# One PSUM tensor of eight banks in place of two rings, a shared exp/mask buffer and a new order, in a windowed attention with a folded feed-forward

## The chip, the cores and the metric

The kernel runs on one core of one Trainium2 chip. The metric is the device time of one launch in microseconds (us); the time given for a kernel is the median of its runs.

## The reference

Sliding-window attention with four sink tokens, and behind it a feed-forward with a product of two branches. Batch 4, 8 heads, 768 positions, head dimension 64; model width 512, inner width 1024; the attention's output, 3072 rows of 512, is the feed-forward's input. Inputs and output are float32.

```python
scores = scale * np.matmul(q, k.transpose(0, 1, 3, 2))
is_sink = pos[None, :] < int(n_sink)              # n_sink = 4
rel = pos[:, None] - pos[None, :]
in_window = (rel >= 0) & (rel < int(window))      # window = 128
scores = np.where(is_sink | in_window, scores, -1000000000.0)
a = np.exp(scores - np.max(scores, axis=-1, keepdims=True))
a = a / (np.sum(a, axis=-1, keepdims=True) + 1e-09)
attn = np.matmul(a, v)
x = attn.transpose(0, 2, 1, 3).reshape(B * S, H * D)
out = (((x @ w1) * (x @ w2)) @ w3) @ w_out
```

## The kernel before, in words

**Tiling.** A batch `b` has 768 positions: three tiles `t` of 256 queries, or six blocks `kb` of 128. The eight heads form four pairs `r`. Products run in bf16 with float32 sums. Because nothing stands between w3 and w_out, the kernel first folds them into one matrix, w3 @ w_out (`w3o`).

**The tasks on TensorE.** Each is a small generator whose first step issues the matmuls and whose later steps issue what other engines do with the result. The plan names them so:

- `t3.i.j`: `fold_w3`, transposes of row block `i` of w3 (line 402). Blocks 0 to 2 come as raw float32 over SP (line 173) and are transposed in two halves of four; the others come through POOL as bf16 (line 131) and take one task of eight transposes.
- `fm.i.n`: `fold_mm`, block `i` of w3 times 128 columns of w_out (line 413), eight matmuls. The four column slices 0 to 3 of w_out are loaded one by one, as ("wo", 0, 128), ("wo", 128, 256) and so on.
- `tpk`, `tpq`: transposes of k and q. Batch 0 uses `transposes_paired` (line 261), two tiles of batch 1 `transposes` (line 233). All later ones are DMA transposes that SP issues (`transposes_dma`, line 270), two for each block: one of k, one of q.
- `sc.b.r.t`: `scores`, the products of k and q of two heads for 256 queries in a tile of two PSUM banks (line 309). ScalarE takes the exponential (line 317), VectorE multiplies with a mask (line 321). Some of these tasks also make the scores of the sink keys (line 303), for two query tiles at once in batches 2 and 3.
- `av.b.r.t`: `values`, probabilities times v, with the row sum in a 65th column (line 343); VectorE takes the reciprocal and scales (lines 347 and 350).
- `sv.b`: `sink_values`, the v rows of the sinks (line 284).
- `xt.b.r.t`: `x_transposes`, transposes of the attention's result (line 360). From batch 1's last tile on, DMA transposes from SP do it (line 370).
- `g.b.c.dt.h`: `gate`, one 128-row block of the first (`h` = 0) or second (1) branch over a chunk `c` of 256 or 384 positions (line 383). ScalarE copies the first branch out into `a_sb` (line 390), VectorE multiplies the second with it (line 387).
- `p.b.m`: `project`, 128 rows of output from `ab` and `w3o` (line 423), copied out by ScalarE or VectorE and stored by SP (line 430). The last one is done in three pieces (`project_pieces`, line 440).

**What sets the order.** `PLAN` lists all 337 TensorE tasks, and TensorE takes them exactly so. The orders of ScalarE, VectorE and SP come out of a small planner that runs while the kernel is built. It gives each step a duration and each load a due time (`arrive`, corrected by `LATER` for batches 2 and 3), and lets each engine take what is ready first. Nothing is decided on the chip: every engine runs its list in order and waits where an input is missing. POOL issues its loads in the order of the list `order`, then q, k and v of batches 1 to 3; no more than eight of its transfers are outstanding.

**PSUM.** There are two pools. `ps_sc` is a ring of two tiles of two banks, for scores alone. `ps_mm` is a ring of four tiles of one bank, for everything else. A ring hands its slots out in turn, so that a task waits for the slot used two, or four, tasks earlier.

**SBUF.** The exponential goes into a tile `ex` (three buffers) and the masked result into a tile `am` (four buffers).

**Filling at the start.** Where the planner sees TensorE idle in the first 40 us, `keep_busy` puts in matmuls whose result is not used (line 458).

Of the kernel before, what the change touches and what calls it, by code (L numbers as in the profile page):

```python
# [21 lines left out]
def kernel(  # L22
# [47 lines left out]
    ps_sc = ctx.enter_context(tc.tile_pool(name="ps_sc", bufs=2, space=PSUM))  # L70
    ps_mm = ctx.enter_context(tc.tile_pool(name="ps_mm", bufs=4, space=PSUM))
# [52 lines left out]
    def load(what, *i):  # L124
# [18 lines left out]
        else:  # L143
# [5 lines left out]
    order = [("w3", 3), ("w3", 4), ("wo", 0, 128), ("wo", 256, 384), ("wo", 384, 512), ("w3", 7), ("q", 0, 0),  # L149
             ("k", 0, 0), ("w3", 6), ("wo", 128, 256), ("k", 0, 1), ("v", 0, 0), ("q", 0, 1), ("q",  # L150
             0, 2), ("w3", 5), ("v", 0, 1), ("k", 0, 2), ("w2", 768, 1024), ("w1", 768, 1024),
             ("w2", 256, 512), ("w1", 256, 512), ("w2", 0, 256), ("w1", 0, 256), ("v", 0, 2), ("w2",
             512, 768), ("w1", 512, 768)] + [
# [74 lines left out]
    def transposes(src, dst, t):  # L228

        tp = ps_mm.tile([P, NP, 2, P], BF16, tag="mm", name="tp")  # L230
        for r in range(NP):
            for i in range(2):
                nc.tensor.transpose(tp[:, r, i, :], src[:, 2 * t + i, r * P:(r + 1) * P],  # L233
                                    ident[:])
        yield
        nc.vector.tensor_copy(dst[:, :, t * 256:(t + 1) * 256],
                              tp[:].rearrange("p r i m -> p r (i m)"))
        yield
# [15 lines left out]
    def transposes_paired(src, dst, t, r0, me):  # L254

        pr = paired(src, t)
        tp = ps_mm.tile([P, 2, 2, P], BF16, tag="mm", name="tp")
        for r in range(2):
            for j in range(2):
# [5 lines left out]
                tp[:].rearrange("p r j m -> p r m j"))  # L265
# [28 lines left out]
    ams = {}  # L294

    def scores(b, r, t, sinks=None):
        c0 = P if t == 0 else 0
        if sinks:
            t0, t1 = sinks
            sp = ps_mm.tile([P, (t1 - t0) * 256], FP32, tag="mm", name="sp")  # L300
            for r_ in range(NP):
                rows = slice(32 * r_, 32 * r_ + 32)
                nc.tensor.matmul(sp[rows, :], ksbd[b][:, r_ * P + 32 * r_:r_ * P + 32 * r_ + 32],  # L303
                                 qT[b][:, r_, t0 * 256:t1 * 256], start=True, stop=True)
        sc = ps_sc.tile([P, 2, 512], FP32, tag="sc", name="sc")
# [7 lines left out]
        if sinks:  # L313
            nc.scalar.activation(es[b][:, (t0 - 1) * 256:(t1 - 1) * 256], sp[:], ACTF.Exp, scale=scale)
            yield
        ex = work.tile([P, 2, 512], BF16, tag="ex", name="ex")
        nc.scalar.activation(ex[:, :, c0:], sc[:, :, c0:], ACTF.Exp, scale=scale)  # L317
        yield
        am = work.tile([P, 2, 512], BF16, tag="am", bufs=4, name="am")
        mk = maskt[:, min(t, 1):min(t, 1) + 1, c0:].to_broadcast([P, 2, 512 - c0])  # L320
        nc.vector.tensor_mul(am[:, :, c0:], ex[:, :, c0:], mk)  # L321
# [5 lines left out]
    def values(b, r, t):  # L327

        am = ams.pop((b, r, t))
        av = ps_mm.tile([P, 2, 2, D + 1], FP32, tag="mm", name="av")  # L330
# [23 lines left out]
    def x_transposes(b, r0, t):  # L354

        me = ("xt", b, r0, t)
        xt = ps_mm.tile([P, 2, 2, P], BF16, tag="mm", name="xt")
# [6 lines left out]
        copy_on(me, xT[b][:, r0:r0 + 2, t * 256:(t + 1) * 256], xt[:].rearrange("p r i m -> p r (i m)"))  # L364
# [11 lines left out]
    def gate(b, c, dt, half):  # L376
# [4 lines left out]
        pg = ps_mm.tile([P, n], FP32, tag="mm", name="pg")  # L381
        for kk in range(NP):
            nc.tensor.matmul(pg[:], w_sb[:, kk, dt * P:(dt + 1) * P], xT[b][:, kk, tk],  # L383
                             start=(kk == 0), stop=(kk == NP - 1))
        yield
        if half:
            nc.vector.tensor_mul(ab[b][:, dt, tk], gate_a.pop((b, c, dt))[:], pg[:])  # L387
        else:
            a_sb = work.tile([P, n], FP32, tag="a_sb", bufs=4, name="a_sb")
            nc.scalar.copy(a_sb[:], pg[:])  # L390
# [5 lines left out]
    def fold_w3(i, j0, j1, me):  # L396
# [3 lines left out]
        tp = ps_mm.tile([P, j1 - j0, P], ty, tag="mm", name="tp3")  # L400
# [5 lines left out]
        copy_on(me, w3T[i][:, j0:j1, :], tp[:])  # L406
        yield

    def fold_mm(i, n0, n1, me):

        po = ps_mm.tile([P, n1 - n0], FP32, tag="mm", name="pw")
        for j in range(KFF):
            nc.tensor.matmul(po[:], w3T[i][:, j, :], wo_sb[:, j, n0:n1],  # L413
                             start=(j == 0), stop=(j == KFF - 1))
        yield
        copy_on(me, w3o[:, i, n0:n1], po[:])
        yield

    def project(b, m):

        po = ps_mm.tile([P, DM], FP32, tag="mm", name="po")
        for kk in range(KFF):
            nc.tensor.matmul(po[:], ab[b][:, kk, m * P:(m + 1) * P], w3o[:, kk, :],  # L423
# [3 lines left out]
        copy_on(("p", b, m), o_sb[:], po[:])  # L427
# [5 lines left out]
    def project_pieces(b, m):  # L433
# [11 lines left out]
        for i in range(3):  # L445
            (nc.scalar.copy if i == 2 else nc.vector.tensor_copy)(o_sbs[i][:], pos[i][:])
# [7 lines left out]
    def keep_busy(n):  # L454

        pz = ps_mm.tile([P, 512], FP32, tag="mm", name="pz")
        for _ in range(n):
            nc.tensor.matmul(pz[:], idle[:, 0:P], idle[:, 0:512], start=True, stop=True)
# [60 lines left out]
    for key in arrive:  # L519
# [7 lines left out]
        t3.0.0 t3.0.4 t3.1.4 t3.1.0 t3.3.0 t3.2.4 t3.2.0 t3.4.0 fm.1.0 fm.4.0 fm.3.0 fm.2.0 fm.4.2  # L527
        fm.1.2 fm.2.2 fm.4.3 fm.0.3 fm.2.3 fm.3.3 t3.7.0 fm.3.2 fm.0.2 fm.0.0 fm.7.3 fm.7.2 fm.7.0
        tpq.0.0.2 tpk.0.0.2 tpk.0.0.0 tpq.0.0.0 fm.1.3 t3.6.0 sc.0.0.0 sc.0.1.0 fm.2.1 fm.4.1 fm.6.0
        fm.7.1 fm.0.1 tpk.0.1.0 tpk.0.1.2 fm.6.3 av.0.0.0 sc.0.2.0 av.0.1.0 fm.3.1 fm.1.1 tpq.0.1.2  # L530
        tpq.0.1.0 xt.0.0.0 av.0.2.0 sc.0.3.0 sv.0 tpq.0.2.0 fm.6.1 t3.5.0 sc.0.0.1 sc.0.1.1 av.0.3.0
        fm.6.2 fm.5.0 fm.5.3 xt.0.2.0 tpk.0.2.2 tpk.0.2.0 tpq.0.2.2 sc.0.2.1 sc.0.3.1 fm.5.2 fm.5.1
        av.0.0.1 g.0.0.7.0 av.0.1.1 g.0.0.7.1 g.0.0.6.0 g.0.0.6.1 xt.0.0.1 sc.0.0.2 sc.0.1.2 g.0.0.3.0
        av.0.2.1 g.0.0.3.1 av.0.3.1 g.0.0.2.0 g.0.0.2.1 g.0.0.1.0 g.0.0.1.1 xt.0.2.1 g.0.0.0.0 sc.0.2.2
        sc.0.3.2 g.0.0.0.1 g.0.1.6.0 g.0.1.7.0 g.0.1.7.1 g.0.1.0.0 g.0.1.0.1 g.0.1.6.1 g.0.0.5.0
        g.0.0.4.0 av.0.0.2 g.0.0.5.1 g.0.1.1.0 g.0.1.1.1 tpk.1.0 g.0.1.2.0 g.0.0.4.1 tpq.1.0 av.0.1.2
        av.0.2.2 av.0.3.2 sc.1.0.0 sc.1.1.0 p.0.1 xt.0.0.2 xt.0.2.2 sc.1.2.0 sc.1.3.0 tpk.1.1 g.0.1.3.0
        g.0.2.0.0 g.0.2.0.1 g.0.1.3.1 g.0.1.2.1 g.0.2.5.0 g.0.2.5.1 g.0.2.2.0 sv.1 g.0.2.4.0 g.0.2.4.1
        tpq.1.1 g.0.2.7.0 g.0.2.2.1 g.0.1.4.0 av.1.0.0 av.1.1.0 sc.1.0.1 sc.1.1.1 av.1.2.0 g.0.2.7.1
        xt.1.0.0 p.0.0 av.1.3.0 g.0.1.4.1 sc.1.2.1 sc.1.3.1 xt.1.2.0 g.0.1.5.0 g.0.1.5.1 g.0.2.3.0  # L540
        g.0.2.6.0 g.0.2.6.1 p.0.3 av.1.0.1 g.0.2.1.0 g.0.2.1.1 g.0.2.3.1 av.1.1.1 av.1.2.1 av.1.3.1
        p.0.5 xt.1.0.1 sc.1.0.2 sc.1.1.2 xt.1.2.1 p.0.4 g.1.0.0.0 g.1.0.6.0 g.1.0.2.0 av.1.0.2 av.1.1.2
        sc.1.2.2 sc.1.3.2 g.1.0.6.1 g.1.0.0.1 g.1.0.7.0 g.1.0.3.0 sc.2.0.0 sc.2.1.0 sv.2 av.1.2.2
        av.1.3.2 g.1.0.7.1 g.1.0.3.1 sc.2.2.0 sc.2.3.0 g.1.0.2.1 g.1.0.1.0 g.1.0.1.1 g.1.0.5.0 av.2.0.0
        g.1.0.5.1 g.1.0.4.0 g.1.0.4.1 p.0.2 p.1.2 av.2.1.0 av.2.2.0 sc.2.0.1 sc.2.1.1 av.2.3.0 p.1.1
        g.1.1.3.0 g.1.1.3.1 g.1.1.1.0 g.1.1.1.1 g.1.1.7.0 g.1.1.7.1 g.1.1.2.0 sc.2.2.1 sc.2.3.1
        g.1.1.2.1 p.1.0 g.1.1.0.0 g.1.1.0.1 av.2.0.1 av.2.1.1 av.2.2.1 av.2.3.1 sc.2.0.2 sc.2.1.2
        g.1.1.4.0 g.1.1.5.0 g.1.1.5.1 g.1.1.4.1 g.1.1.6.0 g.1.1.6.1 sc.2.2.2 sc.2.3.2 av.2.0.2 p.1.3
        av.2.1.2 av.2.2.2 sc.3.0.0 sc.3.1.0 p.1.5 sv.3 av.2.3.2 sc.3.2.0 sc.3.3.0 p.1.4 g.2.0.6.0
        g.2.0.7.0 g.2.0.6.1 g.2.0.3.0 av.3.0.0 g.2.0.3.1 g.2.0.1.0 g.2.0.7.1 g.2.0.5.0 g.2.0.4.0  # L550
        g.2.0.5.1 g.2.0.1.1 g.2.0.0.0 g.2.0.2.0 av.3.1.0 av.3.2.0 av.3.3.0 sc.3.0.1 sc.3.1.1 g.2.0.0.1
        g.2.0.4.1 g.2.1.1.0 g.2.1.0.0 g.2.1.1.1 g.2.0.2.1 g.2.1.2.0 g.2.1.2.1 g.2.1.5.0 g.2.1.5.1 p.2.1
        sc.3.2.1 sc.3.3.1 g.2.1.0.1 g.2.1.4.0 g.2.1.4.1 g.2.1.3.0 g.2.1.3.1 g.2.1.7.0 g.2.1.7.1 av.3.0.1
        av.3.1.1 av.3.2.1 av.3.3.1 sc.3.0.2 sc.3.1.2 g.2.1.6.0 p.2.2 av.3.0.2 sc.3.2.2 sc.3.3.2
        g.2.1.6.1 p.2.0 g.3.0.4.0 g.3.0.7.0 av.3.1.2 av.3.2.2 av.3.3.2 g.3.0.6.0 g.3.0.6.1 p.2.3
        g.3.0.4.1 g.3.0.2.0 g.3.0.2.1 p.2.5 g.3.0.7.1 g.3.1.6.0 g.3.1.0.0 g.3.1.3.0 g.3.1.6.1 g.3.1.2.0
        g.3.1.2.1 g.3.1.0.1 g.3.1.5.0 g.3.1.5.1 g.3.1.3.1 g.3.1.7.0 g.3.1.1.0 g.3.1.1.1 g.3.0.5.0
        g.3.0.5.1 g.3.1.7.1 g.3.0.0.0 g.3.0.0.1 g.3.0.3.0 g.3.0.3.1 g.3.0.1.0 g.3.0.1.1 g.3.1.4.0
# [329 lines left out]
```

The softmax here doesn't subtract the row's maximum and nothing guards it: scores larger than these inputs give would overflow.

## Time and profile before

| | |
|---|---|
| median of 6 runs | 196.75 us (196.51 to 198.68) |
| the profiled execution: its time | 198.68 us |
| its span, first to last instruction | 197.0 us |
| granted TensorE clock, mean | 0.991 |
| TensorE matmul, busy | 188.8 us, 96% of the span |
| VectorE busy | 119.1 us, 60% |
| ScalarE busy | 101.3 us, 51% |
| DMA | 27.58 MB, 140 GB/s in the mean |
| idle of TensorE's matmuls that the profile lays to a DMA | 2.6 us |

A busy matmul row overlaps the next one, so that the 96% say only that TensorE is rarely empty; the spacing of the starts says how fast it goes. The profile names engines PE (TensorE matmul), PEld (its weight loads), DVE (VectorE), ACT (ScalarE), POOL (GpSimd) and SP (SyncE); an SPq or ACTq is the engine's queue. `L383` is line 383 of the kernel. The arrow in `pg<-xT,w_sb` goes from inputs to output.

### The profile page before, as it was taken

To read this page: it belongs to the slowest core of one execution; us is meant where nothing else is said; L and a number is where in the kernel's file an instruction comes from. 1 tells how busy PE (TensorE), PEld (TensorE's weight loads), DVE (VectorE), ACT (ScalarE), POOL (GpSimd) and SP (SyncE) were. 2 spreads that over 40 slices of the span, in tenths; PEclk is the share of its full clock that TensorE was granted. 3 is DMA by queue.
4 is the path that set the end of the run, shared out by engine and by line. 5 is a ranking of instruction groups with operands and counts; after the bars stand their busy time and mean duration, and the time that the engine had idled before them with its cause. 6 is when DMAs were issued, how large, how long until landed. Compare 5 with 4: busy or idle time off the path is not lost.

```text
span 197.0 us, 4859 instructions
## 1 busy us (share of the span) xinstructions
PE 188.8 (96%) x1965; PEld 128.8 (65%) x1978; DVE 119.1 (60%) x285; ACT 101.3 (51%) x180; POOL 74.0 (38%) x98
## 2 busy tenths in 40 slices
PE   6599999999999999999999999999999999999993
PEld 2489988888978677665555656566556565665443
DVE  5254588877887865686673778557457743353212
ACT  2213578878284862684276476637275633323120
POOL 7975667687699563436633330000000000000000
PEclk9979999999999999999999999999999999999999
DMA  6999999999999999999999999999110323000134
GB/s 218 238 188 190 172 180 193 193 177 156 147 147 150 142 131 186 156 215 155 138 139 196 170 185 125 186 173 172 27 57 0 110 82 104 29 3 0 69 147 156
DMA packets 104790, 27.58 MB, mean 140 GB/s; under 512 B 96320, under 2 KB 100800, under 8 KB 104768
## 3 DMA queue, kind: packets, MB, share of 16 engines
q0 software_dynamic: 77744, 13.90, 92.3%
q1 hardware_dynamic: 26880, 13.31, 36.7%
q8 instruction: 15, 0.25, 0.5%
q10 hardware_dynamic: 144, 0.07, 0.1%
q14 instruction: 7, 0.06, 0.1%
HBM read 29.36 MB, written 6.29 MB: 181 GB/s over the span
## 4 chain that ended last, share of the span: by engine, by line
PE 92%; DMA 4%; ACT 1%; issue 1%; DVE 1%; ACTq 0%; POOLq 0%
PE pg L383 42%; PE po L423 20%; PE pw L413 8%; PE av L343 7%; PE sc L309 6%; DMA ab<-in_moe_w_dram 4%; PE tp L402 2%; PE tp L261 2%; PE xt L360 1%; PE tp L233 1%; PE po L440 1%; PE sp L303 1%; PE vp L284 1%; ACT ex L317 0%; DVE ab L387 0%
## 5 line engine op out<-in xcount | busy, mean ns | idle before, releaser
L383 PE MATMUL pg<-xT,w_sb 128*128 128x384 bf16 (+1 forms) x576 | 89.2, 308 | 0.3 <-ACT a_sb L390 0.3
L383 PEld LDWEIGHTS <-w_sb 128*128 128x128 bf16 x576 | 54.5, 98 | 28.0 <-issue 1.5
L387 DVE TENSOR_TENSOR ab<-a_sb,pg 128x384 bf16<-128x384 f32 (+1 forms) x72 | 36.3, 509 | 36.4 <-PE pg L383 33.0
L317 ACT ACTIVATE ex<-sc 128x1024 bf16<-128x1024 f32 (+1 forms) x48 | 44.4, 954 | 13.0 <-PE sc L309 11.3
L390 ACT COPY a_sb<-pg 128x384 f32<-128x384 f32 (+1 forms) x72 | 31.7, 444 | 33.6 <-PE pg L383 26.7
L423 PE MATMUL po<-w3o,ab 128*128 128x512 bf16 x171 | 41.7, 379 | 0.7
L321 DVE TENSOR_TENSOR am<-ex,maskt 128x1024 bf16<-128x1024 bf16 (+1 forms) x48 | 30.2, 642 | 1.6 <-ACT ex L317 1.0
L423 PEld LDWEIGHTS <-ab 128*128 128x128 bf16 x184 | 17.5, 98 | 19.2 <-issue 0.5
L226 ACT COPY o_sb<-po 128x512 f32<-128x512 f32 x18 | 10.5, 586 | 24.9 <-PE po L423 24.9
L350 DVE TENSOR_TENSOR xn<-av,rec 128x256 bf16<-128x256 f32 x48 | 20.4, 425 | 1.7
L115 POOL DMA_DIRECT2D vN<-in_v_dram x18 | 15.9, 886 | 14.3 <-DMA kN<-in_k_dram 11.6
L115 POOL DMA_DIRECT2D kN<-in_k_dram x18 | 16.0, 889 | 11.0 <-DMA qN<-in_q_dram 7.3
L115 POOL DMA_DIRECT2D qN<-in_q_dram x18 | 16.0, 891 | 7.4 <-DMA vN<-in_v_dram 5.0
L343 PE MATMUL av<-vN,am 128*128 128x65 bf16 x352 | 18.2, 193 | 0.0
L343 PEld LDWEIGHTS <-am 128*128 128x128 bf16 x352 | 16.2, 97 | 2.4 <-issue 0.5
L413 PE MATMUL pw<-wo_sb,w3t 128*128 128x128 bf16 x256 | 16.0, 219 | 0.3 <-ACT w3o L226 0.3
L413 PEld LDWEIGHTS <-w3t 128*128 128x128 bf16 x256 | 14.5, 98 | 1.1 <-DVE w3t L226 0.5
L309 PE MATMUL sc<-qT,kT 64*128 64x128 bf16 (+1 forms) x256 | 14.1, 238 | 0.0
L347 DVE RECIPROCAL rec<-av 128x4 f32<-128x4 f32 x48 | 8.5, 177 | 8.1 <-PE av L343 7.8
L343 PE MATMUL av<-vs,es 128*128 128x130 bf16 x64 | 12.1, 220 | 0.0
L402 PE MATMUL tp<-ident,ab 128*128 128x128 bf16 (+1 forms) x64 | 8.1, 298 | 2.6 <-DMA ab<-in_moe_w_dram 2.6
L309 PEld LDWEIGHTS <-kT 64*128 64x128 bf16 x256 | 8.2, 94 | 3.5 <-issue 1.8
(69 smaller groups left out, 119.7 us busy)
## 6 DMA issues: line engine op xcount, KB each, us to landing
out_dram<-o_sb SPq DMA_DIRECT2D x23, 256.0 KB, 5.2
vN<-in_v_dram POOLq DMA_DIRECT2D x24, 128.0 KB, 9.9
kN<-in_k_dram POOLq DMA_DIRECT2D x18, 128.0 KB, 10.6
qN<-in_q_dram POOLq DMA_DIRECT2D x18, 128.0 KB, 11.8
w_sb<-in_moe_w_dram POOLq DMA_DIRECT2D x8, 256.0 KB, 9.4
ab<-in_moe_w_dram SPq DMA_DIRECT2D x3, 512.0 KB, 4.1
ab<-in_moe_w_dram POOLq DMA_DIRECT2D x5, 256.0 KB, 9.7
wo_sb<-in_moe_w_out_dram POOLq DMA_DIRECT2D x4, 256.0 KB, 10.0
```

Source lines behind the costliest of these rows:

```text
L115: nc.gpsimd.dma_start(out=dst, in_=rows(src, b, kb))
L309: nc.tensor.matmul(sc[:, e, c:c + n], kT[b][hp, r, kb * P:(kb + 1) * P], qT[b][hp, r, qb * P:qb * P + n], start=True, stop=True)
L317: nc.scalar.activation(ex[:, :, c0:], sc[:, :, c0:], ACTF.Exp, scale=scale)
L321: nc.vector.tensor_mul(am[:, :, c0:], ex[:, :, c0:], mk)
L343: nc.tensor.matmul(o, lhs, rhs, start=(n == 0), stop=(n == len(todo) - 1), skip_group_check=True)
L350: nc.vector.tensor_mul(xns[b, t][:, :, r, :, :], av[:, :, :, 0:D], rec[:].to_broadcast([P, 2, 2, D]))
L383: nc.tensor.matmul(pg[:], w_sb[:, kk, dt * P:(dt + 1) * P], xT[b][:, kk, tk], start=(kk == 0), stop=(kk == NP - 1))
L387: nc.vector.tensor_mul(ab[b][:, dt, tk], gate_a.pop((b, c, dt))[:], pg[:])
L390: nc.scalar.copy(a_sb[:], pg[:])
L402: nc.tensor.transpose(tp[:, j - j0, :], src[:, j * P:(j + 1) * P], eye[:])
L413: nc.tensor.matmul(po[:], w3T[i][:, j, :], wo_sb[:, j, n0:n1], start=(j == 0), stop=(j == KFF - 1))
L423: nc.tensor.matmul(po[:], ab[b][:, kk, m * P:(m + 1) * P], w3o[:, kk, :], start=(kk == 0), stop=(kk == KFF - 1))
```

## The change

Four things are done together.

1. The two PSUM pools become one tensor `ps` of eight banks. When the planner starts a task, `place` picks the banks: one for most tasks, an aligned pair for scores, one more for sink scores, three for the last projection. It takes those that are clear first, and prefers for a single the partner of a bank in use, so that pairs stay whole. The generator fetches its bank with `bank`.
2. The exponential writes into `am`, and the mask is multiplied in place; `ex` is gone, and `am` has eight buffers. Score tasks no longer wait for the start of the `values` three places earlier but eight places earlier.
3. `order` and `PLAN` are different. Both hold the same loads and the same 337 tasks.
4. The part of `pe_pick` that chose a task when no plan is given is gone, with its constants; `keep_busy` now asks that all banks are clear, and uses the last.

The durations, `LATER`, the due times of DMA transposes and the set of instructions, apart from the buffers, stay as they are.

```diff
-    ps_sc = ctx.enter_context(tc.tile_pool(name="ps_sc", bufs=2, space=PSUM))
-    ps_mm = ctx.enter_context(tc.tile_pool(name="ps_mm", bufs=4, space=PSUM))
+    psum = ctx.enter_context(tc.tile_pool(name="psum", bufs=1, space=PSUM))
+    BANKS = 8
+    ps = psum.tile([P, BANKS, 512], FP32, name="ps")
+    granted = []
+
+    def bank(n, ty=FP32, wide=False):
+
+        at = granted.pop(0)
+        if wide:
+            return ps[:, at:at + 2, :]
+        return (ps[:, at, :] if ty == FP32 else ps[:, at, :].bitcast(ty))[:, 0:n]
...
-    order = [("w3", 3), ("w3", 4), ("wo", 0, 128), ("wo", 256, 384), ("wo", 384, 512), ("w3", 7), ("q", 0, 0),
-             ("k", 0, 0), ("w3", 6), ("wo", 128, 256), ("k", 0, 1), ("v", 0, 0), ("q", 0, 1), ("q",
-             0, 2), ("w3", 5), ("v", 0, 1), ("k", 0, 2), ("w2", 768, 1024), ("w1", 768, 1024),
...
+    order = [("wo", 256, 384), ("wo", 0, 128), ("w3", 3), ("wo", 384, 512), ("w3", 4), ("w3", 7), ("k", 0, 0),
+             ("q", 0, 0), ("w3", 6), ("wo", 128, 256), ("k", 0, 1), ("v", 0, 0), ("q", 0, 1), ("q",
+             0, 2), ("w3", 5), ("k", 0, 2), ("v", 0, 1), ("w2", 768, 1024), ("w1", 768, 1024),
...
-        sc = ps_sc.tile([P, 2, 512], FP32, tag="sc", name="sc")
+        sc = bank(0, wide=True)
...
-        ex = work.tile([P, 2, 512], BF16, tag="ex", name="ex")
-        nc.scalar.activation(ex[:, :, c0:], sc[:, :, c0:], ACTF.Exp, scale=scale)
-        yield
-        am = work.tile([P, 2, 512], BF16, tag="am", bufs=4, name="am")
+        am = work.tile([P, 2, 512], BF16, tag="am", bufs=AM, name="am")
+        nc.scalar.activation(am[:, :, c0:], sc[:, :, c0:], ACTF.Exp, scale=scale)
+        yield
         mk = maskt[:, min(t, 1):min(t, 1) + 1, c0:].to_broadcast([P, 2, 512 - c0])
-        nc.vector.tensor_mul(am[:, :, c0:], ex[:, :, c0:], mk)
+        nc.vector.tensor_mul(am[:, :, c0:], am[:, :, c0:], mk)
...
-        t3.0.0 t3.0.4 t3.1.4 t3.1.0 t3.3.0 t3.2.4 t3.2.0 t3.4.0 fm.1.0 fm.4.0 fm.3.0 fm.2.0 fm.4.2
-        fm.1.2 fm.2.2 fm.4.3 fm.0.3 fm.2.3 fm.3.3 t3.7.0 fm.3.2 fm.0.2 fm.0.0 fm.7.3 fm.7.2 fm.7.0
-        tpq.0.0.2 tpk.0.0.2 tpk.0.0.0 tpq.0.0.0 fm.1.3 t3.6.0 sc.0.0.0 sc.0.1.0 fm.2.1 fm.4.1 fm.6.0
...
-        g.0.2.6.0 g.0.2.6.1 p.0.3 av.1.0.1 g.0.2.1.0 g.0.2.1.1 g.0.2.3.1 av.1.1.1 av.1.2.1 av.1.3.1
-        p.0.5 xt.1.0.1 sc.1.0.2 sc.1.1.2 xt.1.2.1 p.0.4 g.1.0.0.0 g.1.0.6.0 g.1.0.2.0 av.1.0.2 av.1.1.2
...
+        t3.0.4 t3.1.0 t3.0.0 t3.2.4 t3.2.0 t3.1.4 fm.0.2 fm.2.2 fm.1.0 fm.0.0 fm.2.0 t3.3.0 fm.1.2
+        fm.0.3 fm.3.2 fm.2.3 t3.4.0 fm.1.3 t3.7.0 fm.3.0 fm.4.3 fm.4.0 fm.7.3 fm.7.2 fm.3.3 fm.7.0
+        tpk.0.0.2 tpk.0.0.0 tpq.0.0.0 tpq.0.0.2 fm.4.2 t3.6.0 sc.0.0.0 sc.0.1.0 sc.0.2.0 fm.1.1 fm.6.1
...
+        av.1.0.1 av.1.1.1 g.0.2.7.1 sc.1.2.1 sc.1.3.1 p.0.3 p.0.5 av.1.2.1 av.1.3.1 sc.1.0.2 sc.1.1.2
+        xt.1.2.0 xt.1.0.1 xt.1.2.1 p.0.4 g.1.0.7.0 g.1.0.7.1 g.1.0.0.0 av.1.0.2 sc.1.2.2 sc.1.3.2
...
                      started=([("sc",) + unit[-1]] if unit else [])
-                     + ([("av",) + unit[-3]] if lead and len(unit) > 3 else []))
+                     + ([("av",) + unit[-AM]] if len(unit) >= AM else []))
...
+    def place(widths, est):
+
+        taken, at = [], {}
+        for w in sorted(set(widths), reverse=True):
+            for n in [n for n, x in enumerate(widths) if x == w]:
+                best = None
+                for i in range(0, BANKS, w):
+                    mine = range(i, i + w)
+                    if any(x in taken or clear[x] is None for x in mine):
+                        continue
+                    ready = max(clear[x] for x in mine) + HOP
+                    other = i ^ 1
+                    whole = w == 1 and other not in taken and clear[other] is not None and clear[other] + HOP <= est
+                    key = (max(ready, est), whole, -ready, i)
+                    if best is None or key < best:
+                        best = key
+                if best is None:
+                    return None
+                at[n] = best[3]
+                taken += range(best[3], best[3] + w)
+                est = max(est, best[0])
+        return est, [at[n] for n in range(len(widths))]
```

## The prediction

> **What bounds the kernel now.** I read the page's engine shares first, then the table of stretches, the start of the timeline, and last the waits of TensorE's weight loads and of SP.
>
> ```profile
> PE 188.8 (96%) x1965; PEld 128.8 (65%) x1978; DVE 119.1 (60%) x285; ACT 101.3 (51%) x180; POOL 74.0 (38%) x98
> ...
> PEclk9979999999999999999999999999999999999999
> ```
>
> TensorE is the bound: VectorE and ScalarE have about half of the span free. The clock row has one dip, in the third slice (about 10 to 15 us). The table of stretches (us; then PE, PEld, DVE, ACT, POOL, clock, DMA) says where PE's slack lies:
>
> ```profile
> 9.33:13.66 4.33, 3.99 (x32) 3.76 (x33) 2.13 (x4) 0.85 (x2) 3.43 (x7) 0.61 1.78 187
> 13.66:21.36 7.70, 7.70 (x137) 7.60 (x138) 3.25 (x13) 2.12 (x8) 4.58 (x7) 1.00 1.61 187
> 21.36:77.70 56.34, 56.10 (x810) 45.81 (x812) 44.48 (x110) 37.87 (x73) 40.89 (x50) 1.00 2.05 164
> 77.70:182.00 104.30, 103.63 (x899) 62.17 (x909) 61.83 (x142) 55.98 (x91) 16.92 (x20) 1.00 1.03 116
> ```
>
> After 13.66 us PE is full. The mean length of a matmul counts its pipeline, so I took the spacing of starts in the trace: 0.163 us for a 384-column gate matmul, 0.216 for 512 columns, 0.109 for 256, 0.056 for 128. With these a gate task is 0.651 us (0.437 with 256 columns), a projection 1.727, a fold 0.445, a `values` 0.357 (0.181 at t=0). The 337 tasks of the plan sum to 177.6 us, and 59 changes between score, paired-transpose and full-array tasks, at 0.1 each, add 5.9: 183.5. The last projection thus comes out at 191.6 us where the trace has it at 192.07: **PE's real stalls after the start are only 0.5 us**. What can be won lies in the start, the changes of tiling and the tail. The start on the timeline:
>
> ```profile
> 4.27 2.71 PE L402 MATMUL tp<-ident,ab 128*128 128x128 f32 x16 [0.20 <-DMA ab<-in_moe_w_dram]
> 9.33 3.54 PE L402 MATMUL tp<-ident,ab 128*128 128x128 bf16 x24 [2.35 <-DMA ab<-in_moe_w_dram]
> 12.71 0.61 PE L413 MATMUL pw<-wo_sb,w3t 128*128 128x128 bf16 x8
> 13.66 4.64 PE L413 MATMUL pw<-wo_sb,w3t 128*128 128x128 bf16 x80 [0.34 <-ACT w3o L226]
> ...
> 21.36 0.41 PE L261 MATMUL tp<-ident,qN 128*64 128x128 bf16 x8
> ```
>
> PE sits 2.35 us until w3 row block 3 lands (`t3.3.0`), works at half clock until 12.7, and starts the folds (`pw`) only at 12.71. The waits, in us in total, times, longest, of TensorE's weight loads and then of SP's queue:
>
> ```profile
> PEld L402 <- DMA ab<-in_moe_w_dram: 2.6, 1, 2.6
> ...
> PEld L303 <- DMA qT<-qN: 0.3, 1, 0.3
> ```
> ```profile
> SPq L270 <- DMA kN<-in_k_dram: 6.4, 3, 5.0
> ```
> ```profile
> 65.12 2.55 SPq L270 DMA_TRANSPOSE kT<-kN  x2
> 67.77 3.82 SPq L270 DMA_TRANSPOSE qT<-qN  x2
> ```
>
> Small, but they decide this case: at two places PE meets a DMA transpose with nothing to spare. `sc.1.0.2` starts at 77.70 us; its last input, the transpose of q(1,5) (batch 1, block 5), landed at 77.61. `sc.2.2.1` starts at 105.84; q(2,5) landed at 105.55. q(1,5) is late because SP, after two transposes at 57.25 and 58.65, stands 5.0 us on k(2,0), which lands at 65.03, though k(1,5) had landed at 59.80; behind it SP issues k(2,0), k(1,5), q(2,0), q(1,5), the last at 70.27, and 7.3 us later it lands.
>
> **What the Trainium skill says.** "DMA: Bandwidth & Descriptors" (Queues, rings and completion order) has each DMA engine take turns between the queues that have work, by packets. The trace agrees in kind: the three raw w3 loads, issued within 1 us on SP, took 3.3, 4.1 and 8.1 us, the third beside POOL's loads. "TensorE: Matmul & The Clock Gate" (Part 1) halves the clock after an idle window of some 3.4 us; here the half clock holds from 9.27 to 12.68, just after the 2.35 us of idling. "TensorEngine Tiling" (Array Packing; Key Properties) says that a change of tiling mode drains the array: here a gate task's last matmul before scores stands 0.205 us against 0.109, the last score matmul 0.15 against 0.03. "PSUM — Partial Sum Buffer" (PSUM bank collisions) keeps engines apart by bank, so a single tensor loses nothing if waits follow banks; no run here shows that yet.
>
> **The change part by part.** (1) *Start.* POOL's first six loads are the same six, reordered; w3 block 7 stays sixth. They landed at 9.28, 10.83, 12.27, 13.69, 15.21 and 16.44, so I keep these for the positions. The plan now folds raw blocks 0 to 2 against wo 256:384 (first) and wo 0:128 (second) before any POOL-loaded w3 block. Folds then start near 9.5 instead of 12.7. What ends last is w3 block 7: `t3.7.0` at 16.4 (0.45), then seven folds (7 x 0.445 = 3.1): the first paired transposes at 19.95 against 21.36. The same three bf16 and six fp32 transpose tasks and 17 folds lie before it in both, so **PE leads by 1.4 us**. A half clock from 9.3 to 12.7 would not alter it: about 1.5 us of catching up is available before 16.4. The bounds: 0.3, should raw block 2 land at 9.87 as now and all six slip by 1 us; 2.0 if they come earlier. The next inputs landed 2.0 to 2.7 us ahead of their use (k(0,0) 19.30 for 21.6, w3 block 6 20.61 for 22.89, v 25.21 for 27.24), so the lead can be used there.
>
> (2) *Banks.* Eight single banks replace four singles plus two pairs. No instruction is added. In before one slot wait is visible: a gate at 92.86 idle 0.25 us, behind an `a_sb` copy that stood behind an exp. At most 8 score results live without their `values` against 4. Gain 0.3 to 0.4 us; loss 0 to 1 if three score tasks in a row (3 x 1.03 us of exp) hold six banks and the copies queue behind them.
>
> (3) *Shared exp/mask buffer.* The same 48 exp (1.025 us) and 48 multiplies (0.686), in place. Not seen before; bounds: minus 5 to plus 10% of 30.2 us of DVE, hidden by DVE's 40% idle. I take 0.
>
> (4) *Order.* 22 stretches of score tasks instead of 25, 52 changes of tiling for 59: 7 x 0.1 = 0.7 us, 0.1 before `sc.1.0.2`, 0.6 after.
>
> (5) *SP and POOL.* The same DMAs. The planner ranks transposes by arrival and `LATER` is unchanged, so k(2,0) stays ahead of k(1,5). POOL issues back to back there (0.87 us each from 50.45), and waits on landings, not on PE: **q(1,5) lands at 77.6 again**.
>
> The sum: PE would reach `sc.1.0.2` at 75.5: 1.4 from the start, 0.1 from a change of tiling, 0.45 since the plan puts two x transposes behind it, and 0.2 of stalls. It finds q(1,5) missing and stands 2 us, with everything queued behind on PE. After that, against before: -0.6 (six changes), +0.45 (two tasks of 0.224 that now come later), -0.3 (the slot wait), -0.1 (q(2,5)): **-0.55**. Span 197.0 to 196.4, the profiled execution's 198.68 to 198.1. That execution is the slowest of six; the difference carries over to the median: 196.75 to 196.2, and as small new stalls and an earlier SP queue pull either way I say 196.1. Half a per cent is 1.0 us, about what a measurement of this kernel can tell from no change.
>
> **The rivals.** *The lead is kept.* If q(1,5) comes 2 us sooner, because stores and loads fall otherwise at 57 to 65 us or SP's order turns, then -1.4 - 0.7 - 0.4 = -2.5: 194.3. For it: all compute inputs have slack. Against: POOL and SP are bound by landings there.
>
> *SP is blocked by stores (slower).* The new order is laid out for an earlier PE; once PE has stood at 77.6, each store and x transpose that SP holds ahead of a k or q transpose comes later too. In before SP stands from 84.5 to 89.1 for x of (1,2), with k(2,4) landed at 87.25. If this grows by 2 us, q(2,5) lands at 107.5 and `sc.2.2.1` (105.5 in the new order) stands 2 us; less the 0.55: 198.2. It decides from the point where q(2,5) is later than 105.5 + 0.5. Against: `p.1.0` is the only new store ahead of `sc.2.2.1`, and (1,2) is finished at 87.7 against 87.9.
>
> *The banks aren't told apart.* If a matmul waited for every reader of the one tensor, each of 337 tasks would see an eviction of 0.3 to 0.7 us: over 250 us.
>
> **How the numbers follow.** Lead taken back at q(1,5): 0.50, at 196.1, its own range 195.2 to 197.0; of it 0.14 is beyond -0.5%, 0.34 within, 0.02 slower. Lead kept: 0.29, all faster. Stores: 0.18 (0.17 slower, 0.01 within). Banks: 0.03. Faster 0.43, same 0.35, slower 0.22. The range reaches to 193.9 (the kept lead with the start's better bound) and 198.3.
>
> **What would show it.** Right: first paired transpose near 20 us; no gate waiting for `a_sb`; a wait of PE or PEld on qT of 1 to 2.5 us near 77 us. Kept lead: no such wait, `sc.1.0.2` near 75.5. Wrong altogether: first paired transpose after 21, or waits on ACT or DVE of over 1 us between 20 and 75 us.

## The result, and the profile after

The kernel after takes 197.11 us in the median (196.07 to 198.75, 33 runs), the kernel before 196.56 us (196.30 to 198.68, 70 runs). The ratio of after to before is **1.0024 [1.0014, 1.0035]**: a little slower, and by less than the half per cent that the prediction called "about what a measurement of this kernel can tell from no change". The profiled execution of after took 197.29 us, its span is 195.6 us. Its runs also scatter more: the middle half of them lies between 196.66 and 197.46 us, that of before between 196.50 and 196.68.

The page of after, engine shares and clock row:

```profile
PE 187.7 (96%) x1965; PEld 126.5 (65%) x1978; DVE 117.8 (60%) x284; ACT 101.3 (52%) x181; POOL 74.0 (38%) x98
...
PEclk9999999999999999999999999999999999999999
```

TensorE is still the bound, and the dip in the clock is gone. The table of stretches of after, cut where that of before was cut (the first paired transposes, `sc.1.0.2`, and 10 us ahead of the last projection); columns are us, then PE, PEld, DVE, ACT, POOL, clock, DMA:

```profile
9.33:13.66 4.33, 3.80 (x61) 3.28 (x60) 2.43 (x9) 1.55 (x5) 3.54 (x7) 1.00 1.40 200
13.66:19.75 6.09, 5.95 (x104) 5.67 (x102) 2.55 (x6) 1.59 (x6) 3.64 (x5) 1.00 1.55 189
19.75:76.91 57.16, 55.78 (x801) 45.13 (x803) 42.93 (x109) 38.38 (x73) 40.86 (x50) 1.00 2.02 163
76.91:180.69 103.78, 103.31 (x904) 61.69 (x913) 62.92 (x144) 54.20 (x88) 17.79 (x21) 1.00 1.06 121
```

The third line is the one to read: 57.16 us, of which PE was empty for 1.4. In the first profile of before this stretch was 56.34 with 0.24 empty. The start of after on TensorE's timeline:

```profile
8.02 1.53 PE L410 MATMUL ps<-ident,ab 128*128 128x128 f32 x12 [0.69 <-DMA ab<-in_moe_w_dram]
9.38 1.20 PE L421 MATMUL ps<-wo_sb,w3t 128*128 128x128 bf16 x16
...
16.08 0.62 PE L410 MATMUL ps<-ident,ab 128*128 128x128 bf16 x8
16.53 3.29 PE L421 MATMUL ps<-wo_sb,w3t 128*128 128x128 bf16 x56
19.75 0.64 PE L270 MATMUL ps<-ident,kN 128*64 128x128 bf16 x16
```

The folds start at 9.38, `t3.7.0` at 16.08 and the paired transposes at 19.75, against 21.36 in the first profile of before. The same view shows where PE was empty later:

```profile
29.00 0.28 PE L312 MATMUL ps<-qT,ksbd 128*32 128x256 bf16 x1
29.93 0.29 PE L312 MATMUL ps<-qT,ksbd 128*32 128x256 bf16 x3 [0.64 <-DVE qT L235]
...
76.91 0.29 PE L312 MATMUL ps<-qT,ksbd 128*32 128x256 bf16 x4 [0.58 <-DMA qT<-qN]
```

Line 312 makes the sink scores. The first of four such matmuls goes at 29.00 and the second 0.93 us later, behind a VectorE copy into `qT` (`sc.0.0.1`). At 76.91 `sc.1.0.2` starts 0.74 us late, behind the transpose of q(1,5), which landed at 76.87. (The brackets are smaller than the gaps between the starts, since they leave out the pipeline of the matmul before.) The waits of TensorE's weight loads and of SP's queue on loads have become shorter:

```profile
PEld ps L410 <- DMA ab<-in_moe_w_dram: 1.5, 2, 1.0
```
```profile
SPq L279 <- DMA kN<-in_k_dram: 1.9, 1, 1.9
```

They were 2.6 and 6.4 us in the first profile of before. SP thus waits less for data here, and all the same q(1,5) comes late; the section on the prediction shows for what.

### The profile page after: what moved, and what is told of

Its sections match the earlier page's. It is cut to its first block, busy times and chain, and to the rows that moved or that the text cites. A ratio compares the mean times of both kernels' runs of the same rounds, so it can differ in the third digit from the quotient of the medians.

```text
span 195.6 us, 4888 instructions
## 1 busy us (share of the span) xinstructions
PE 187.7 (96%) x1965; PEld 126.5 (65%) x1978; DVE 117.8 (60%) x284; ACT 101.3 (52%) x181; POOL 74.0 (38%) x98
## 4 chain that ended last, share of the span: by engine, by line
PE 59%; DMA 28%; POOL 10%; issue 2%; ACT 0%; POOLq 0%
PE ps L391 32%; PE ps L431 17%; DMA qN<-in_q_dram 6%; DMA w_sb<-in_moe_w_dram 5%; DMA qT<-qN 5%; DMA ab<-in_moe_w_dram 5%; PE ps L351 5%; DMA vN<-in_v_dram 4%; PE ps L318 4%; DMA kN<-in_k_dram 3%; POOL qN L124 2%; POOL vN L124 2%; POOL kN L124 2%; POOL wo_sb L130 1%; PE ps L448 1%
## 5 line engine op out<-in xcount | busy, mean ns | idle before, releaser
L391 PE MATMUL ps<-xT,w_sb 128*128 128x384 bf16 (+1 forms) x576 | 90.5, 308 | 0.0
L395 DVE TENSOR_TENSOR ab<-a_sb,ps 128x384 bf16<-128x384 f32 (+1 forms) x72 | 36.5, 508 | 26.7 <-PE ps L391 22.8
L398 ACT COPY a_sb<-ps 128x384 f32<-128x384 f32 (+1 forms) x72 | 31.9, 443 | 37.8 <-PE ps L391 28.7
L326 ACT ACTIVATE am<-ps 128x1024 bf16<-128x1024 f32 (+1 forms) x48 | 44.3, 957 | 4.8 <-PE ps L318 4.7
L431 PE MATMUL ps<-w3o,ab 128*128 128x512 bf16 x171 | 41.3, 379 | 0.6
L329 DVE TENSOR_TENSOR am<-am,maskt 128x1024 bf16<-128x1024 bf16 (+1 forms) x48 | 29.8, 641 | 4.6 <-ACT am L326 4.5
L358 DVE TENSOR_TENSOR xn<-ps,rec 128x256 bf16<-128x256 f32 x48 | 20.4, 424 | 1.7
L351 PE MATMUL ps<-vN,am 128*128 128x65 bf16 x352 | 18.4, 193 | 0.0
L421 PE MATMUL ps<-wo_sb,w3t 128*128 128x128 bf16 x256 | 17.1, 219 | 0.5 <-DMA wo_sb<-in_moe_w_out_dram 0.5
L318 PE MATMUL ps<-qT,kT 64*128 64x128 bf16 (+1 forms) x256 | 13.5, 238 | 0.0
```

The costliest lines, as they stand in the source:

```text
L318: nc.tensor.matmul(sc[:, e, c:c + n], kT[b][hp, r, kb * P:(kb + 1) * P], qT[b][hp, r, qb * P:qb * P + n], start=True, stop=True)
L326: nc.scalar.activation(am[:, :, c0:], sc[:, :, c0:], ACTF.Exp, scale=scale)
L329: nc.vector.tensor_mul(am[:, :, c0:], am[:, :, c0:], mk)
L351: nc.tensor.matmul(o, lhs, rhs, start=(n == 0), stop=(n == len(todo) - 1), skip_group_check=True)
L358: nc.vector.tensor_mul(xns[b, t][:, :, r, :, :], av[:, :, :, 0:D], rec[:].to_broadcast([P, 2, 2, D]))
L391: nc.tensor.matmul(pg, w_sb[:, kk, dt * P:(dt + 1) * P], xT[b][:, kk, tk], start=(kk == 0), stop=(kk == NP - 1))
```

## The experiments

### Before again, and the change without its orders

The first run is before once more, unchanged, for a second profile.

> The kernel before, unchanged, in a second profiled execution. The one shown took 198.68 us, 2.1 us over the median of 196.56. Theory A (the half clock from 9.27 to 12.68 us belongs to that execution): span near 194.9 us, mean clock 1.0, first paired transposes before 20.5 us instead of 21.36, so that most of the start gain that the prediction counted for the change is there already. Theory B (the start is as in the first profile and the 2.1 us lie elsewhere, in the transfers): half clock again, first paired transposes at 21.4, and another landing of q(1,5) than 77.6.

It took 196.47 us (span 194.7), and its start is another one:

```profile
7.63 0.62 PE L402 MATMUL tp<-ident,ab 128*128 128x128 bf16 x8 [1.16 <-DMA ab<-in_moe_w_dram]
9.10 1.51 PE L402 MATMUL tp<-ident,ab 128*128 128x128 f32 x16 [0.85 <-DVE w3t L226]
10.89 5.29 PE L413 MATMUL pw<-wo_sb,w3t 128*128 128x128 bf16 x88 [0.29 <-DVE w3t L226]
16.02 0.61 PE L402 MATMUL tp<-ident,ab 128*128 128x128 bf16 x8
16.47 2.84 PE L413 MATMUL pw<-wo_sb,w3t 128*128 128x128 bf16 x48
19.24 0.41 PE L261 MATMUL tp<-ident,qN 128*64 128x128 bf16 x8
```

w3 block 3 is there at 7.58 instead of 9.28, PE idles 1.16 us instead of 2.35, no half clock follows, and the paired transposes start at **19.24**, half a microsecond ahead of after's. That is the first of the two theories. The 2.1 us by which the first profiled execution of before was late at this point are the 2.1 us by which it was above the median.

Next, the banks and the shared buffer alone. The kernel is after with before's `order` and `PLAN`:

```diff
-    order = [("wo", 256, 384), ("wo", 0, 128), ("w3", 3), ...
+    order = [("w3", 3), ("w3", 4), ("wo", 0, 128), ("wo", 256, 384), ...
-        t3.0.4 t3.1.0 t3.0.0 t3.2.4 t3.2.0 t3.1.4 fm.0.2 fm.2.2 ...
+        t3.0.0 t3.0.4 t3.1.4 t3.1.0 t3.3.0 t3.2.4 t3.2.0 t3.4.0 ...
```

> The changed kernel with the load order and the plan of before: only the eight banks and the shared exp/mask buffer remain. Theory A (banks and buffer are neutral, because PE in before waits for a slot only once): 0.997 to 1.001 of before. Theory C (the banks or the shared buffer cost, by waits that the single tensor adds or by a slower in-place multiply): 1.002 or more, and DVE's multiply above 0.70 us or new waits of PE on ACT or DVE.

196.42 us, ratio 0.9999 [0.9984, 1.0014], as expected by theory A; its profiled span is 194.4. The slot wait is gone. TensorE's timeline of before (second profile), and then of this kernel at the same gates:

```profile
90.61 2.11 PE L383 MATMUL pg<-xT,w_sb 128*128 128x384 bf16 x12 [0.25 <-ACT a_sb L390]
```
```profile
90.31 2.11 PE L391 MATMUL ps<-xT,w_sb 128*128 128x384 bf16 x12
```

The exponential keeps its length, 954 ns in both pages, and so does the multiplication with the mask, 642 ns.

The loads and the plan of the order, one without the other:

```diff
 # after with before's loads, PLAN of after
-    order = [("wo", 256, 384), ("wo", 0, 128), ("w3", 3), ...
+    order = [("w3", 3), ("w3", 4), ("wo", 0, 128), ("wo", 256, 384), ...
```

> The changed kernel with the load order of before and the new plan. The new plan asks for w_out columns 256 to 383 first, which in the old order land fourth, at 13.7 us. Theory A (what comes before 77 us is bound by the transposes, so a start that is later by up to 2 us is mostly hidden): 1.000 to 1.006 of before, with no wait for q(1,5). Theory D (the start counts fully): 1.010 or more.

200.04 us, ratio 1.0184 [1.0163, 1.0205]: theory D. The folds of the new plan want wo 256:384, which now comes fourth; the paired transposes start at 21.75, 2.0 us later than in after, and from there to `sc.1.0.2` it is 57.88 us against 57.16, with a wait of 1.4 us for a masked `am` that ends at 30.18. Together that is the 2.7 us by which its span (198.3) is longer. So a late start counts in full here.

```diff
 # after with before's PLAN, loads of after
-        t3.0.4 t3.1.0 t3.0.0 t3.2.4 t3.2.0 t3.1.4 fm.0.2 fm.2.2 ...
+        t3.0.0 t3.0.4 t3.1.4 t3.1.0 t3.3.0 t3.2.4 t3.2.0 t3.4.0 ...
```

> The changed kernel with the plan of before, but the new load order. Theory A: the old plan asks for w3 block 3 early, which now lands third; the start is later by some 1.5 to 3 us, and some of it is hidden where PE stands at q(1,5): 1.002 to 1.012. If q(1,5) bounds what comes before 77 us, the ratio stays within 1.003 in spite of the later start.

203.16 us, ratio 1.0310 [1.0270, 1.0351], far outside what was expected. The old plan needs w3 block 3 as its fifth task, and in the new list it is the third load. TensorE's timeline of this kernel:

```profile
11.68 2.74 PE L410 MATMUL ps<-ident,ab 128*128 128x128 bf16 x16 [4.94 <-DMA ab<-in_moe_w_dram]
```

The clock then stands at a half from 11.51 to 14.92 us, and the paired transposes start only at 24.36. This profiled run (201.26 us, mean clock 0.991) is one of the two fastest; the other four list a mean clock of 0.973 to 0.975. So loads and plan are one thing at the start: neither half can be judged by itself.

### Four attempts to take the two waits away

```diff
 # PLAN: the task that waits at 29.00 goes two tasks later
-        ... tpq.0.2.0 sc.0.0.1 t3.5.0 fm.6.2 av.0.3.0 ...
+        ... tpq.0.2.0 t3.5.0 fm.6.2 sc.0.0.1 av.0.3.0 ...
```

> The changed kernel; sc.0.0.1 is moved two places down its plan, behind t3.5.0 and fm.6.2, so that the copy of q which it waits 0.9 us for at 29 us is done. Theory A (two waits in series: what is saved at 29 us is waited for again at q(1,5), 0.74 us in the profile of after, which would grow to about 1.5): unchanged, within 0.3 us of the changed kernel, 1.001 to 1.004 of before. Theory E (the wait at 29 us costs its full length): 0.9 us faster, 0.998 of before.

198.01 us, ratio 1.0081 [1.0053, 1.0109]: slower than both theories had it. The sink scores run through, but PE stands at the same place for something else. TensorE's timeline, and the waits of its weight loads between 27 and 31 us:

```profile
28.22 0.41 PE L270 MATMUL ps<-ident,qN 128*64 128x128 bf16 x8
29.43 0.62 PE L410 MATMUL ps<-ident,ab 128*128 128x128 bf16 x8 [0.80 <-DVE qT L235]
...
30.43 0.29 PE L312 MATMUL ps<-qT,ksbd 128*32 128x256 bf16 x4
```
```profile
PEld L410 <- DMA ab<-in_moe_w_dram: 1.0, 1, 1.0
```

The matmul row blames the copy into `qT`. That copy ended at 29.44, after the matmul had started; w3 block 5, which `t3.5.0` transposes, landed at 29.39. So the row of the weight load is the one to believe, and the wait has only changed its name. At `sc.1.0.2` nothing was waited for again: q(1,5) landed at 74.59, 1.9 us ahead of its use.

```diff
 # SP leaves the store of p.0.1 behind the transposes
-            queue[e].append((at + HOP, YIELD.get(k["name"][0], 0.1), us, k))
+            wait = 6.0 if e == "sp" and k["name"] == ("p", 0, 1) else YIELD.get(k["name"][0], 0.1)
+            queue[e].append((at + HOP, wait, us, k))
```

> The changed kernel; only SP's queue is altered, with the store of the first projection (p.0.1) behind the DMA transposes of batch 1's last tile instead of ahead of them. In the profile of after, SP holds the transpose of k(1,4) 1.9 us for that store although its data have landed. Theory A (the store ahead makes q(1,5) late): q(1,5) lands 1.5 to 3 us earlier, PE's wait for it of 0.6 us goes, 0.7 us faster than the changed kernel: 0.998 to 1.000 of before. Theory F (q(1,5) is late because of bandwidth): landing and time as in after.

197.99 us, ratio 1.0076 [1.0058, 1.0094]: the time is not what theory A forecast, but its landing is. The edit does what it says: q(1,5) lands at 73.82, 3.1 us earlier than in after, and `sc.1.0.2` no longer waits. But SP's later order changes more than this: at 125.04 a gate stands for a bank out of which ScalarE has not yet copied a projection, where after had no wait (TensorE's timeline of this kernel):

```profile
125.04 1.14 PE L391 MATMUL ps<-xT,w_sb 128*128 128x384 bf16 x6 [0.67 <-ACT o_sb L235]
```

Both edits together, with the same two pieces of diff:

> Both edits, sc.0.0.1 two places later and the store behind the transposes. Theory A: both waits go, 1.5 us faster than the changed kernel: 0.993 to 0.997 of before. If only one of the two counts, 0.998 to 1.000. If new waits on transposes come in their place, 1.000 or more.

198.63 us, ratio 1.0094 [1.0069, 1.0120]: nothing of the 1.5 us came, and the third case of the expectation did. The wait of 0.67 us at the gate is there again (at 123.91), and q(1,5) lands only at 76.33, just ahead of `sc.1.0.2`, although the store stands behind: k(2,0) landed at 62.77 here, against 61.28 with the store alone moved, and SP stands for it. And both edits with the start of before:

```diff
 # up to w3 block 6 in the loads, up to t3.6.0 in the plan: as before
-    order = [("wo", 256, 384), ("wo", 0, 128), ("w3", 3), ...
+    order = [("w3", 3), ("w3", 4), ("wo", 0, 128), ("wo", 256, 384), ...
-        t3.0.4 t3.1.0 t3.0.0 t3.2.4 ... fm.4.2 t3.6.0 ...
+        t3.0.0 t3.0.4 t3.1.4 t3.1.0 ... fm.1.3 t3.6.0 ...
```

> As with both edits, and the first eight loads and the plan up to the first paired transposes are those of before. Theory A (the new loads' start is 0.5 us later than that of before in a typical execution, since the two w_out slices at the head land with a late last engine): another 0.5 us, 0.990 to 0.995 of before, first paired transposes at 19.2 us. If what comes before 77 us is bound by transposes that start from loads at a fixed time, no better than with both edits alone.

197.07 us, ratio 1.0030 [1.0018, 1.0042]: not the gain of 0.5 to 1 per cent that was expected. It has a new wait of 1.4 us in front of the `values` at 28.05, for a masked `am`, and still comes out 1.6 us below the run with both edits, with half of its runs within 0.3 us. That points at the start as the source of the scatter. What it does not explain is why the medians of the first three lie 0.9 to 1.5 us above after's, while the profiled spans of two of them (195.2 and 195.9) do not; those profiles were among their own fastest executions, and where the slower ones lose is open.

### Moving the other task, and the start once more

In these experiments the wait at 29.00 was approached from the wrong side. Sink score two of four reads columns 1024 to 1280 of a partition of `qT` (pair 1, query tile 1). The copy that it waits for writes query tile 2 of pairs 0 and 1, that is 512 to 768 and 1280 to 1536: no column in common, but 512 to 1536 taken as one range encloses the read. The first sink score, at 256 to 512, lies outside it and did not wait. That the wait was set for this reason is argued from which of the four waited, not shown. So the next kernel moves the transposes of tile 2 behind the scores:

```diff
-        ... fm.3.1 tpq.0.2.0 sc.0.0.1 t3.5.0 fm.6.2 ...
+        ... fm.3.1 sc.0.0.1 tpq.0.2.0 t3.5.0 fm.6.2 ...
```

> The kernel after, with one task moved: the paired transposes of query tile 2 (tpq.0.2.0) go behind the scores of tile 1 (sc.0.0.1) instead of in front of them. Theory 'span of the copy': the second sink-score matmul of sc.0.0.1 waits 0.92 us for the copy of tile 2 although it reads tile 1, because the copy's range of qT (512 to 1536 of each partition) encloses it; with the copy behind it the wait goes. sc.0.0.1 runs through from about 28.8, no wait over 0.3 us follows before w3 block 5, and the median is 0.5 to 0.9 us below that of after: ratio to before 0.998 to 1.000. Rival 'loads': as in the run that moved sc.0.0.1, PE then stands for w3 block 5 (landing near 29), or for q(1,5) at sc.1.0.2, and what goes at one place comes back at the other: ratio 1.002 to 1.006.

196.93 us, ratio 1.0009 [0.9991, 1.0027]. The wait is gone (TensorE's timeline of this kernel):

```profile
28.25 0.29 PE L312 MATMUL ps<-qT,ksbd 128*32 128x256 bf16 x4 [0.17 <-ACT qT L235]
28.48 0.40 PE L318 MATMUL ps<-qT,kT 64*128 64x128 bf16 x6
...
92.50 0.56 PE L318 MATMUL ps<-qT,kT 64*128 64x256 bf16 x10 [1.17 <-DMA qT<-qN]
```

But 1.37 us come back at 91 us, where PE now meets a later q transpose of SP that it had not caught up with before. Both theories are half right: the wait can be avoided, but in this execution the transfers ate most of what was won.

Then after twice more, unchanged, for one profile each:

> The kernel after again, for one more execution and its profile. Theory 'late DMA engine': what differs from execution to execution is how far one DMA engine falls behind in the first software loads (in the profiled execution the last piece of the first wo load landed 1.15 us behind the median piece, 9.32 against 8.17, and all loads to 29 us kept that distance). The first paired transposes start as much earlier or later as w3 block 7 lands (16.03 in the profile of after), and the time moves with it, at least half of it. Rival: the start is the same within 0.2 us and the difference in time arises behind 30 us.

> The same once more, so that three executions of after stand beside each other; the same two theories with the same numbers.

They took 197.17 and 197.70 us. With them there are eight profiled executions with the new list of loads (one of them with the old plan) and six with the old list; the table has ten of them. This table is worked out from the trace's landing records, for w3 block 7, the sixth of POOL's loads: when its median piece (the trace has sixteen landings for each load) landed, when the last, and when the paired transposes began.

| execution | median piece | last piece | paired transposes |
|---|---|---|---|
| after | 14.82 | 16.03 | 19.75 |
| after, second profile | 14.77 | 15.73 | 19.45 |
| after, third profile | 15.16 | 16.47 | 20.77 |
| `sc.0.0.1` later | 14.69 | 15.60 | 19.32 |
| store later | 14.99 | 16.11 | 20.41 |
| both | 14.87 | 15.78 | 19.50 |
| transposes of tile 2 later | 14.71 | 15.12 | 18.85 |
| before, first profile | 14.91 | 16.44 | 21.36 |
| before again | 14.74 | 15.02 | 19.24 |
| banks alone | 14.75 | 15.00 | 19.30 |

The median piece moves by less than 0.5 us. The last one moves by 1.4 us in the seven rows with the new start, and its lag is there from the first load on. The theory speaks of one DMA engine. In the first profile of before it is indeed one piece of sixteen that is late; with the new list it is mostly several (five are over 0.4 us behind the median in after, four in its third profile), and the trace does not say which engine brought which.

In the rows with the new start, PE begins the paired transposes 3.72 us after that landing, and 4.30 us after it in the two where it had idled for 1.7 and 1.5 us before and the clock fell for a while (mean clock 0.991 and 0.989). TensorE's timeline of after's third profile, where the clock stands at a half from 9.01 to 12.42 us:

```profile
8.51 2.39 PE L410 MATMUL ps<-ident,ab 128*128 128x128 f32 x12 [1.68 <-DMA ab<-in_moe_w_dram]
```

With the old list the last piece is 0.2 to 0.3 us late in five of six executions, and 1.5 in the one that was profiled first; with the new list it is 0.4 to 1.3 late. Expected was that at least half of the shift reaches the end; between the second and third profile it was less, 0.53 of 1.32 us, since in the second PE stood 0.7 us in the middle of a task at 27 us, for nothing that the profile shows, and in both `sc.1.0.2` then met q(1,5). Why the pieces are late with the new list was not tried.

Last, the front of before with the back of after, in the new banks. It is the kernel "banks alone" with

```diff
 # PLAN: before's up to sc.1.0.2, from there what is left in after's order
-        ... p.0.5 xt.1.0.1 sc.1.0.2 sc.1.1.2 xt.1.2.1 p.0.4 g.1.0.0.0 g.1.0.6.0 g.1.0.2.0 ...
+        ... p.0.5 xt.1.0.1 sc.1.0.2 sc.1.1.2 xt.1.2.1 p.0.4 g.1.0.7.0 g.1.0.7.1 g.1.0.0.0 ...
```

> The banks and the shared buffer of after, the loads of before, the order of before up to sc.1.0.2 and that of after from there. Theory: the loss of after lies ahead of sc.1.0.2 (start, copy wait, q(1,5)), its gain behind it (113.8 us from sc.1.0.2 to the last projection, against 114.4 in before and 114.0 with the banks alone). So the median is 0.1 to 0.4 us below that of the banks alone, 196.0 to 196.3, ratio 0.997 to 0.999, and the runs scatter as little as before's (most within 0.5 us). Rival: the shorter back needs the front that it was searched with, and new waits eat it: ratio 1.000 to 1.003.

195.57 us (195.46 to 195.96), ratio **0.9959 [0.9946, 0.9972]**: faster than both kernels, more than expected. Its stretches of TensorE:

```profile
19.36:75.62 56.26, 56.25 (x812) 45.89 (x811) 44.11 (x110) 37.86 (x73) 40.81 (x50) 1.00 1.99 169
75.62:178.96 103.34, 103.34 (x907) 61.25 (x906) 63.05 (x143) 54.13 (x88) 17.85 (x21) 1.00 1.05 120
```

In 159.6 us from the paired transposes on PE is empty for 0.01 us. This kernel has neither of after's two waits, and the back of after without them.

## Why the prediction was right and wrong

Cut at four tasks, the profiled executions add up like this (us; the first column is when the paired transposes start, the next three are lengths):

| kernel | start | to `sc.1.0.2` | to `sc.3.0.0` | to `p.3.5` | span |
|---|---|---|---|---|---|
| before, first profile | 21.36 | 56.34 | 42.23 | 72.14 | 197.0 |
| before again | 19.24 | 56.20 | 42.23 | 72.14 | 194.7 |
| banks alone | 19.30 | 56.25 | 41.83 | 72.14 | 194.4 |
| after | 19.75 | 57.16 | 41.70 | 72.08 | 195.6 |
| after, second profile | 19.45 | 57.31 | 41.70 | 72.08 | 195.5 |
| after, third profile | 20.77 | 56.52 | 41.70 | 72.08 | 196.0 |
| old front | 19.36 | 56.26 | 41.26 | 72.08 | 193.9 |

In after, two x transposes (0.45 us) stand behind `sc.1.0.2`; in the others they stand ahead of it. Like for like its second column is 57.61 and its third 41.25. In the last four rows one `values` task (`av.2.2.2`, 0.36 us) stands behind `sc.3.0.0`; in the first three it stands ahead of it.

**(1) The start: right for the kernel after, wrong in what it was measured against.** Folds near 9.5 (9.38), `t3.7.0` at 16.4 (16.08) and the first paired transposes at 19.95 (19.75, 19.45, 20.77) came as worked out. But "PE leads by 1.4 us" took 21.36 from the one profile at hand. With before's order and loads the start is 19.24 to 19.36 in the three other profiles, so after has no lead. It lags by 0.1 to 1.5 us. **This is the step that failed**, and with it the sentence "the difference carries over to the median": the profiled execution's 2 us over the median lay exactly in the stage that the change rebuilds, so that a difference formed inside that execution could not be carried over.

The prediction had the two kernels level at `sc.1.0.2`, since q(1,5) takes the lead back; against before again, after comes there 1.92 us later, like for like. The table of landings tells what became of the lead. Behind the landing of w3 block 7 the new plan needs 3.72 us, the old one 4.22 to 4.32 in those three profiles: it does lead, by half a microsecond. But with the new list that landing came at 15.73 to 16.47 in after, not at the 15.00 to 15.04 of the old one. Where it came at 15.12 (transposes of tile 2 later), the start was 18.85 and ahead of before's. Nor does "a half clock from 9.3 to 12.7 would not alter it" hold: twice such a clock cost 0.58 us.

**(2) Banks: right.** 0.3 to 0.4 us were predicted; in the profiles 42.23 to 41.83 is 0.40, all of it at the gate shown above (90.61 against 90.31 us, though banks alone comes to `sc.1.0.2` 0.11 us later), and no gate waits for the copy into `a_sb` any more. The medians of the runs are too blunt to show it (0.9999). "The banks aren't told apart" is refuted by every run.

**(3) Shared buffer: right**, no change to be seen in either operation. (Of the 48 of each, 32 have the lengths that the prediction gives; the 16 of the first query tile are shorter.)

**(4) Order: right behind `sc.1.0.2`.** 0.6 us for six changes of tiling were predicted there. Banks alone to old front is 0.57 plus 0.06 = 0.63, and the profile shows no wait of PE there in either kernel. With the `values` task on the same side it is 0.21 up to `sc.3.0.0`, where the new order has two changes fewer, and 0.42 behind it, where it has four fewer: 0.1 us each at both places. The whole of the back was put at -0.6 - 0.3 - 0.1 = -1.0, and is -1.03 in the old front.

**(5) SP and POOL: wrong in mechanism, and its number belonged to the wrong execution.** "q(1,5) lands at 77.6 again" was read from the late execution; in before again it lands at 74.23, 1.2 us ahead of its use. That it lands within 0.8 us of the predicted time in after is luck: the cause that the prediction gave, SP standing 5.0 us for k(2,0), is not there, since k(2,0) landed at 61.80 instead of 65.03. And PE waits 0.74 us for it, less than the 1 to 2.5 us named. Yet in after SP does depend on PE. SP's timeline of after, then of before again:

```profile
58.38 0.35 SPq L438 DMA_DIRECT2D out_dram<-o_sb  x1
58.77 1.52 SPq L279 DMA_TRANSPOSE kT<-kN  x1
...
64.94 5.29 SPq L279 DMA_TRANSPOSE qT<-qN  x2
```
```profile
54.48 0.35 SPq L430 DMA_DIRECT2D out_dram<-o_sb  x1
56.25 1.42 SPq L270 DMA_TRANSPOSE kT<-kN  x1
...
64.21 4.11 SPq L270 DMA_TRANSPOSE qT<-qN  x2
```

The first row of each is the store of `p.0.1`, which the new plan puts at 55.84 instead of 51.93. k(1,4) had landed at 56.91 and stands behind it until 58.77. The queue behind it is late as well, though not by as much: k(2,0) is issued 0.48 us later than in before again, where SP stands 2.4 us for it, q(1,5) 1.65 us later, after longer issues on the way. It lands at 76.87. So a chain runs from PE over a store to SP and back to PE; what shows it is the run with the store moved, where q(1,5) landed at 73.82. It is one way to a late q(1,5) and not the only one, as the run with both edits has it. The chain is the mechanism of the rival "SP is blocked by stores", at another place and with 0.7 us instead of 2. In the second and third profile of after q(1,5) landed at 76.71 and 77.25, and `sc.1.0.2` followed 0.05 us later, with PE hardly waiting.

**What no step had:** the 0.92 us at 29.00. It was in every profiled execution that kept the new plan there. The prediction's list of what would prove it wrong allowed only for waits of over 1 us between 20 and 75.

The sum, against before again: start +0.51, then +1.41 (0.92 and 0.74 of waits, less what small things give back), then -1.04: +0.88, where the spans give 0.9. That the two waits cost these times is read from the profiles: of the four kernels with the new start that took one or both away, only the one with the transposes of tile 2 later came out below after, by 0.18 us in the median, which is within the noise. What the last kernel shows is that the front as a whole loses and the back gains. The medians, over all runs, differ by 0.55. Had the prediction known a typical before, its own step of "PE stands 2 us at q(1,5)" would have cost time instead of only taking back a lead.

## What to carry to other kernels

Before a difference is formed inside one profiled execution, ask in which stage that execution differs from its kernel's median; if the change touches that stage, the difference does not carry over, and a clock dip and a last DMA piece 1.5 us behind the median piece are signs of it. A change of several parts can hold a gain in its back and lose it in its front: splitting it by time, at a task that both orders share, found a kernel better than both where splitting it by kind (loads, plan) made only worse ones. And where a wait is taken away, look for the input that is next to arrive: here w3 block 5 landed within 0.1 us of the end of the copy that was avoided (29.39 and 29.44), and a q transpose of SP took back 1.4 us of what another edit had won.

## What the hardware showed that was not expected

- Pieces of a load that fall behind in the first 8 us can stay behind by the same amount for 20 us: in after the last pieces landed 1.15, 1.21 and 1.13 us behind the median ones at 9.3, 16.0 and 28.9 us. How far they fall varied from 0.4 to 1.3 us between executions with the same list of loads. A start without lag is no promise: in before again the last piece is 0.3 us late up to the seventh load, and 1.2 from the eighth on.
- Behind idle times of 1.68 us (third profile of after) and 1.54 us (store later), which ended at 8.51 and 8.13 us, the clock fell to a half, and the paired transposes came 0.58 us later than the landing alone would have given (4.30 against 3.72). Of the fourteen profiles, the five in which TensorE idled for 1.54 us or more at once between 4 and 12 us have a half clock there, of 3.41 us each; the nine with 1.18 us or less have none. The Trainium skill, "TensorE: Matmul & The Clock Gate" (Part 1), as named in the prediction, gives an idle window of some 3.4 us before the clock falls; in four of the five the idling was shorter (1.54 to 2.35 us), and for this kernel the measured times decide.
- From `sc.1.0.2` on the kernel repeats to the hundredth: 41.70 and 72.08 us in all three executions of after. All of its scatter in these three profiles is made in the first 77 us.
